# Attention scores by blocks of 64 tokens with both heads on 128 partitions, in a fused attention and expert kernel

## The chip, the cores and the metric

One core of a Trainium2 chip. The time is device time in microseconds of one launch, median of several runs. TensorE is called PE in the profile, its weight loads PEld, VectorE DVE, ScalarE ACT, GpSimd POOL, SyncE SP.

## The reference

```python
def _attn_ref(q, k, v):                       # 4 x 8 heads x 576 tokens x 64, float32
    scores = 1/sqrt(64) * q @ k.T
    mask = (pos[:, None] // 64) >= (pos[None, :] // 64)
    scores = np.where(mask, scores, -1e9);  scores -= scores.max(-1)
    attn = np.exp(scores);  attn /= attn.sum(-1) + 1e-9
    return attn @ v
x = attention as 2304 tokens x 512
x = leaky_relu(x @ w_in, 0.01) @ w_out        # 512 x 2048, 2048 x 512
out = top-1 of 8 experts with a skip score    # w1 512 x 1024, w2 1024 x 512 each
```

A token sees all tokens of its own block of 64 and of the blocks before it. 576 tokens are nine blocks.

## The kernel before

The kernel has four stages: attention, into which the first quarter of the first layer ("half a", 512 of 2048 hidden columns) is woven; the rest of that layer; routing with the first expert; the other experts. The change is in the attention (`class Attention`, lines 28 to 285) and in the due times of the steps woven into it (line 448).

The attention works on 16 pairs of heads, four pairs for each of four batch entries. For a pair, `load` brings q, k and v with tokens on partitions (tiles `qn`, `kn`, `vn`; five tiles of 128 tokens, the last half full). `prep` turns k and q with TensorE (`transposes`, lines 89 to 95; the last 64 tokens by a transpose of 64 rows and columns) into PSUM tile `big`; ACT copies k (line 98), DVE copies q times the scale (line 113). Head 0 stands on partitions 0 to 63, head 1 on 64 to 127. POOL copies the last 64 tokens of q into the diagonal quarters of `qd`, zero elsewhere (line 116).

`s_steps` makes the scores. `products` (line 126) takes a tile of 128 query tokens j = 0 to 3 against 128 (j + 1) keys, one float32 matmul per head with 64 rows of contraction; each is two MATMUL instructions. A small bf16 product adds -1e30 where the first 64 queries would see the last 64 keys (line 133). `soft` takes the row maximum (DVE, line 143) and the exponential with its sum (ACT, line 144), `norm` divides (DVE, then POOL, line 152). `rest` (line 177) does the last 64 tokens, both heads at once, with `qd` and K of 128.

`t_steps` transposes the probabilities P by 128x128 (line 205), copies them out of PSUM by turns with ACT and DVE (line 207; tile `ph`), and multiplies with the values (`mm`, line 241: per head 64 output partitions, tile `pv`); `fin` splits the result in two float32r halves in `xT`. Steps with g = 0 cover tokens 0 to 255, with g = 1 tokens 256 to 575.

Order: `steps` (line 256) gives each step a due time, two units to a pair; the transposes and values of a pair come `1 + lag` = 2.3 units behind its scores, so that neighbouring pairs overlap. The steps of half a and the splitting of its weights (`split64`) have due times of their own, and line 466 runs all in order of due time. A planner then orders each engine's instructions by a simulated timeline; `keep_in_program_order` ties an instruction behind the one traced before it on its engine. PSUM tags: `ps` has four banks (scores and transposed P), `mm` two (values, half a), `big` one double bank.

Of the kernel before, what the change touches and what calls it, by code (L numbers as in the profile page):

```python
# [27 lines left out]
class Attention:  # L28
# [3 lines left out]

    MASK = -1e30

    def __init__(self, tc, ctx, q, k, v, ident, ps, side, place):
        nc = self.nc = tc.nc  # L40
        self.q, self.k, self.v, self.ident, self.ps = q, k, v, ident, ps
        self.B, self.H, self.S, self.D = q.shape
        S = self.S
        self.nt = nt = S // 128
        self.pool = ctx.enter_context(tc.tile_pool(name="at", bufs=2, side=side))
        fix = ctx.enter_context(tc.tile_pool(name="afix", bufs=1, side=side))

        self.nat = [fix.tile([128, 5, 2, 64], F32, name=nm) for nm in ("qn", "kn")]
        self.qT, self.kT = ([place[:, S * i : S * i + S] for i in at] for at in ((0, 1), (2, 3)))
        self.mask = [fix.tile([128, n], BF16, name=nm) for nm, n in (("who", 128), ("mask", 64))]  # L50
        nc.vector.memset(self.mask[0], 0.0)
        for h in range(2):
# [8 lines left out]
        self.P2 = []
        for i in range(2):
            self.P2.append([fix.tile([128, 2, 128 * (j + 1)], F32, name=f"P{j}_{i}") for j in range(nt)])
            t = fix.tile([128, 128 * (nt + 1)], F32, name=f"P{nt}_{i}")
            nc.gpsimd.memset(t[:, S:], 0.0)
            self.P2[i].append(t)
# [16 lines left out]
    def prep(self, p, nat):  # L83
        nc, S = self.nc, self.S
        qn, kn = nat
        qT, kT, qd = self.qT[p % 2], self.kT[p % 2], self.qd[p % 2]
        st = dict(qT=qT, kT=kT, qd=qd, vs=self.vn[p % 3])

        def transposes(src):
            pt = self.ps.tile([128, 1024], F32, name="big", bufs=1)  # L90
            f = src.rearrange("p t h d -> p t (h d)")
            for t in range(4):
                nc.tensor.transpose(pt[:, t * 128 : (t + 1) * 128], f[:, t], self.ident)  # L93
            nc.tensor.transpose(pt[:, 512:576], f[0:64, 4], self.ident[0:64, 0:64])
            return pt[:, 0:S]

        def s_k():
            nc.scalar.copy(kT, transposes(kn))

        def s_q():  # L100
            if p:
                parts = [(transposes(qn), 0, S)]
            else:
                f = qn.rearrange("p t h d -> p t (h d)")
                parts = []
                for i0, i1 in ((0, 512), (512, S)):
                    pt = self.ps.tile([128, 512], F32, name="pq", tag="mm", bufs=2)
                    for t in range(i0 // 128, -(-i1 // 128)):
                        m = min(128, i1 - 128 * t)
                        nc.tensor.transpose(pt[:, 128 * t - i0 : 128 * t - i0 + m], f[0:m, t], self.ident[0:m, 0:m])  # L110
                    parts.append((pt[:, 0 : i1 - i0], i0, i1))
            for pt, i0, i1 in parts:
                nc.vector.tensor_scalar(out=qT[:, i0:i1], in0=pt, scalar1=self.D ** -0.5, scalar2=None, op0=ALU.mult)
            for h in range(2):
                r = slice(64 * h, 64 * h + 64)
                nc.gpsimd.tensor_copy(qd[r, r], qT[r, S - 64 : S])

        return st, [s_k, s_q]

    def s_steps(self, p, st, g):  # L120
# [5 lines left out]
        def products(sp, j, c0):  # L126
            n = 128 * (j + 1)
            for h in range(2):
                r = slice(64 * h, 64 * h + 64)
                nc.tensor.matmul(sp[h][:, c0 : c0 + n], st()["qT"][r, 128 * j : 128 * j + 128], st()["kT"][r, 0:n], start=True, stop=False)  # L130
            for h in range(2):
                r = slice(64 * h, 64 * h + 64)
                nc.tensor.matmul(sp[h][:, c0 + n - 64 : c0 + n], self.mask[0][r], self.mask[1][r], start=False, stop=True)  # L133
# [20 lines left out]
        def pair():  # L154
            return [self.ps.tile([128, 512], F32, name="sp", tag="ps", bufs=4) for _ in range(2)]

        def both():
            sp = pair()
            st_ = stat("both", 4)
            for j in range(2):  # L160
                products(sp, j, 128 * j)
            for j in range(2):
                for h in range(2):
                    soft(Ps[j][:, h], sp[h][:, 128 * j : 128 * j + 128 * (j + 1)], st_, 2 * j + h)
            norm([Ps[i][:, h] for i in range(2) for h in range(2)], st_)

        def one(j):
            n = 128 * (j + 1)
            sp = pair()
            products(sp, j, 0)  # L170
            st_ = stat(f"one{j}", 2 if j < self.nt - 1 else 3)
            for h in range(2):
                soft(Ps[j][:, h], sp[h][:, 0:n], st_, h)
            if j < self.nt - 1:
                norm([Ps[j][:, i] for i in range(2)], st_)

        def rest():

            n, S = self.S // 2, self.S
            sp = self.ps.tile([128, 1024], F32, name="big", bufs=1).rearrange("p (a c) -> p a c", a=2)  # L180
            for a in range(2):
                nc.tensor.matmul(sp[:, a, 0:n], st()["qd"], st()["kT"][:, a * n : a * n + n], start=True, stop=True)  # L182
            P = Ps[self.nt][:, 0:S]
            j = self.nt - 1
            st_ = stat(f"one{j}", 3)
            soft(P.rearrange("p (a c) -> p a c", a=2), sp[:, :, 0:n], st_, 2, AX.XY)
            norm([Ps[j][:, i] for i in range(2)] + [P], st_)

        if g == 0:
            return [both]  # L190
        return [lambda j=j: one(j) for j in range(2, self.nt)] + [rest]

    def t_steps(self, p, st, g, xh, xl):
# [3 lines left out]
        last = Ps[self.nt]  # L197
# [14 lines left out]
        def four(jc):  # L212

            js = (2 * g, 2 * g + 1)
            turn(lambda pt: [(pt[:, (2 * h + i) * 128 : (2 * h + i + 1) * 128], Ps[j][:, h, jc * 128 : jc * 128 + 128])
                             for h in range(2) for i, j in enumerate(js)],
                 lambda t, pt: (t[:, jc, :, 0:256], pt.rearrange("p (h c) -> p h c", h=2)), "ad"[jc % 2])

        def second():
            turn(lambda pt: [(pt[:, h * 128 : h * 128 + 128], Ps[1][:, h, 128:256]) for h in range(2)],  # L220
                 lambda t, pt: (t[:, 1, :, 128:256], pt[:, 0:256].rearrange("p (h c) -> p h c", h=2)), "d")

        def fourth():
            def todo(pt):
                v = pt[:, 0:384].rearrange("p (h c) -> p h c", h=2)
                return [(v[:, h, 0:128], Ps[3][:, h, 384:512]) for h in range(2)] + [(v[:, :, 128:192], last[:, 384:512])]
            turn(todo, lambda t, pt: (t[:, 3, :, 0:192], pt[:, 0:384].rearrange("p (h c) -> p h c", h=2)), "a")
# [5 lines left out]
        if g == 0:  # L233
            turns = [lambda: four(0), second]

            runs = [(0, 0, slice(0, 256), 0), (1, 1, slice(128, 256), 128)]
        else:
            turns = [lambda jc=jc: four(jc) for jc in range(3)] + [fourth, lasts]
            runs = [(jc, jc, slice(0, 320), 0) for jc in range(3)] + [(3, 3, slice(0, 192), 128), (4, 3, slice(256, 320), 256)]

        def mm(run):
            jc, i, cs, c0 = run
            if jc == 0:
                box["pv"] = self.ps.tile([128, 512], F32, name="pv", tag="mm", bufs=2)
# [9 lines left out]
        return [alloc] + turns + [lambda run=run: mm(run) for run in runs] + [fin]  # L254

    def steps(self, dst, lag):
# [17 lines left out]
        for p in range(pairs):  # L274
# [14 lines left out]
def attention_moe_kernel(  # L289
# [158 lines left out]
    for u, (t0, t1, n) in enumerate(((10.35, 17.15, 7), (17.15, 19.1, 4), (21.5, 26.2, 7), (26.35, 33.1, 7))):  # L448
# [277 lines left out]
    lag = 2  # L726
# [628 lines left out]
```

## Time and profile before

| | |
|---|---|
| median of 3 runs | 803.55 us (801.63 to 805.36) |
| profiled execution | 804.18 us, span 802.4 us |
| mean granted clock of TensorE | 0.984 |
| PE busy | 762.4 us (95%), 4526 instructions |
| PEld, DVE, ACT, POOL busy | 579.9, 426.3, 331.7, 309.3 us |
| chain that ended last | PE 78%, DVE 12%, DMA 3% |

Busy time of PE is that of overlapping, pipelined matmuls: an instruction's own duration is longer than its distance to the next one. The price of an instruction in a full stream is the distance between starts. A row `MATMUL sp<-wbt 64*128 64x384` has 64 rows of contraction, 128 columns of the stationary operand and 384 columns that stream; `x4` counts instructions merged into the row.

### The profile page before, as it was taken

To read this page: it belongs to the slowest core of one execution; us is meant where nothing else is said; L and a number is where in the kernel's file an instruction comes from. 1 tells how busy PE (TensorE), PEld (TensorE's weight loads), DVE (VectorE), ACT (ScalarE), POOL (GpSimd) and SP (SyncE) were. 2 spreads that over 40 slices of the span, in tenths; PEclk is the share of its full clock that TensorE was granted. 3 is DMA by queue.
4 is the path that set the end of the run, shared out by engine and by line. 5 is a ranking of instruction groups with operands and counts; after the bars stand their busy time and mean duration, and the time that the engine had idled before them with its cause. 6 is when DMAs were issued, how large, how long until landed. Compare 5 with 4: busy or idle time off the path is not lost.

```text
span 802.4 us, 12709 instructions
## 1 busy us (share of the span) xinstructions
PE 762.4 (95%) x4526; PEld 579.9 (72%) x4527; DVE 426.3 (53%) x1030; ACT 331.7 (41%) x783; POOL 309.3 (39%) x427
## 2 busy tenths in 40 slices
PE   4799999999999999999999999999999998899995
PEld 2456776777766769899989998878899976674441
DVE  2786554454535664576574299996912365221121
ACT  3786555564545665555454222122222251111221
POOL 2785442343424352554344333435332452201011
PEclk8799999999999999999999999999999999999998
DMA  7464622262122031662224356302302221999630
GB/s 170 120 177 104 177 46 71 58 176 72 45 81 48 16 106 40 213 231 82 86 79 158 79 158 197 119 26 93 119 2 79 54 91 30 311 348 388 238 128 14
DMA packets 101108, 96.91 MB, mean 121 GB/s; under 512 B 69198, under 2 KB 72270, under 8 KB 101042
## 3 DMA queue, kind: packets, MB, share of 16 engines
q1 hardware_dynamic: 93778, 82.58, 33.2%
q0 software_dynamic: 7264, 13.50, 5.7%
q8 instruction: 36, 0.59, 0.3%
q14 instruction: 30, 0.25, 0.1%
HBM read 74.38 MB, written 21.98 MB: 120 GB/s over the span
## 4 chain that ended last, share of the span: by engine, by line
PE 78%; DVE 12%; DMA 3%; issue 2%; ACT 2%; SPq 2%; POOL 1%; POOLq 0%; DVEq 0%; ACTq 0%
PE ph L389 21%; PE acc L389 13%; PE sp L130 7%; PE po L389 7%; DVE xlast L608 6%; PE pv L246 6%; PE pt L205 5%; PE ph L1119 3%; PE pp L1133 3%; PE big L182 2%; PE py L861 2%; PE big L93 2%; PE ph L861 1%; DMA list<-li,sli 1%; DVE u L380 1%
## 5 line engine op out<-in xcount | busy, mean ns | idle before, releaser
L389 PE MATMUL ph<-xT,wbt 128*128 128x384 f32 x864 | 167.1, 338 | 4.2 <-DVE u L380 3.1
L389 PEld LDWEIGHTS ph<-xT,wbt 128*128 128x128 f32 x864 | 151.8, 188 | 14.0 <-DVE u L380 5.1
L381 POOL TENSOR_TENSOR gl<-u,gh 128x384 fp32r<-128x384 f32 x72 | 80.4, 1117 | 138.9 <-ACT gh L380 130.9
L389 PE MATMUL acc<-wbt,gh 128*128 128x512 f32 x432 | 131.9, 394 | 0.0
L152 POOL TENSOR_SCALAR P<-P,stat 128x128 f32<-128x128 f32 (+2 forms) x144 | 81.4, 584 | 88.2 <-DVE stat L150 69.2
L389 PEld LDWEIGHTS acc<-wbt,gh 128*128 128x128 f32 x432 | 79.7, 188 | 12.0
L380 ACT CAST gh<-u 128x384 fp32r<-128x384 f32 x72 | 37.0, 514 | 120.8 <-DVE u L380 52.0
L389 PE MATMUL acc<-wbt,gl 128*128 128x512 f32 x216 | 82.1, 396 | 0.0
L143 DVE TENSOR_REDUCE stat<-sp 128x1 f32<-128x128 f32 (+3 forms) x128 | 60.1, 485 | 40.6 <-PE sp L133 28.8
L144 ACT ACTIVATE P<-sp,stat 128x128 f32<-128x128 f32 (+3 forms) x128 | 67.5, 531 | 28.3 <-DVE stat L143 27.4
L380 DVE TENSOR_TENSOR u<-ph,u 128x384 f32<-128x384 f32 x72 | 39.7, 551 | 70.4 <-ACT u L379 70.2
L130 PE MATMUL sp<-wbt 64*128 64x128 f32 (+3 forms) x256 | 72.4, 496 | 1.2 <-ACT P L144 0.7
L379 ACT ACTIVATE u<-ph 128x384 f32<-128x384 f32 x72 | 35.3, 490 | 63.9 <-PE ph L389 55.8
L205 PE MATMUL pt<-ident,P 128*128 128x128 f32 x400 | 60.0, 282 | 0.2 <-ACT P L144 0.2
L360 POOL TENSOR_TENSOR cv<-cv,cv 128x512 int32<-128x512 int32 x32 | 41.5, 1297 | 44.8 <-DVE cv L359 32.7
L389 PE MATMUL ph<-xT,wia 128*128 128x384 f32 x288 | 57.3, 344 | 0.0
L246 PE MATMUL pv<-ph,vn 128*64 128x320 f32 (+4 forms) x448 | 53.6, 367 | 2.1 <-ACT ph L207 1.2
L205 PEld LDWEIGHTS pt<-ident,P 128*128 128x128 f32 x400 | 45.4, 142 | 13.9 <-issue 8.6
L389 PE MATMUL po<-woa,gA 128*128 128x512 f32 x216 | 54.6, 400 | 0.0
L608 DVE CUSTOM_DVE_ANT_0 xlast<-x,raw 128x512 f32<-128x512 f32 x72 | 53.7, 785 | 0.0
L389 PEld LDWEIGHTS ph<-xT,wia 128*128 128x128 f32 x288 | 49.1, 188 | 4.0 <-issue 0.9
L389 PEld LDWEIGHTS po<-woa,gA 128*128 128x128 f32 x216 | 39.4, 188 | 11.6 <-issue 1.8
(264 smaller groups left out, 1120.7 us busy)
## 6 DMA issues: line engine op xcount, KB each, us to landing
wbt<-in_moe_w_dram SPq DMA_DIRECT2D x40, 512.0 KB
raw<-in_moe_w_in_dram SPq DMA_DIRECT2D x16, 512.0 KB
raw<-in_moe_w_out_dram SPq DMA_DIRECT2D x16, 512.0 KB
xTd<-xT POOLq DMA_DIRECT2D x4, 1152.0 KB
part_d<-cv SPq DMA_DIRECT2D x18, 256.0 KB
x<-part_d SPq DMA_DIRECT2D x6, 768.0 KB
xT<-xTd POOLq DMA_DIRECT2D x6, 768.0 KB
out_dram<-x SPq DMA_DIRECT2D x6, 768.0 KB
```

The costliest lines, as they stand in the source:

```text
L130: nc.tensor.matmul(sp[h][:, c0 : c0 + n], st()["qT"][r, 128 * j : 128 * j + 128], st()["kT"][r, 0:n], start=True, stop=False)
L143: nc.vector.tensor_reduce(out=st_[:, 1, i : i + 1], in_=sv, op=ALU.max, axis=ax, negate=True)
L144: nc.scalar.activation(out=P, in_=sv, func=AF.Exp, bias=st_[:, 1, i : i + 1], accum_out=st_[:, 0, i : i + 1])
L152: nc.gpsimd.tensor_scalar(out=P, in0=P, scalar1=rs[:, i : i + 1], scalar2=1.0, op0=ALU.mult, op1=ALU.mult)
L205: nc.tensor.transpose(o, src, self.ident)
L246: nc.tensor.matmul(box["pv"][64 * h : 64 * h + 64, c0:N], st()["vs"][:, jc, h], box["ph"][:, i, h, cs], start=(jc == 0), stop=(jc == runs[ ...
L360: nc.gpsimd.tensor_tensor(out=w, in0=w, in1=low, op=ALU.add)
L379: nc.scalar.activation(out=u, in_=ph, func=AF.Copy, scale=0.01)
L380: return [nc.vector.tensor_tensor(out=u, in0=ph, in1=u, op=ALU.max), nc.scalar.copy(gh, u), nc.gpsimd.tensor_tensor(out=gl, in0=u, in1=gh. ...
L381: nc.gpsimd.tensor_tensor(out=gl, in0=u, in1=gh.bitcast(F32), op=ALU.subtract)]
L389: nc.tensor.matmul(ps, x, y, start=first and m == 0, stop=last and m == 3 * n - 1)
L608: nc.vector.tensor_tensor_reduce(out=junk, in0=x2[:, t], in1=wrow[j], scale=1.0, scalar=0.0, op0=ALU.mult, op1=ALU.add, accum_out=box["L"] ...
```

## The change

The scores are made by blocks of 64 queries. `qd` now holds all nine blocks of q: block i has head 0's 64 queries in columns 0 to 63 on partitions 0 to 63, head 1's in columns 64 to 127 on partitions 64 to 127, and zeros in the other quarters. One matmul with 128 rows of contraction gives both heads' scores of block j, on 128 partitions, against exactly 64 (j + 1) keys: no mask. The scaled q goes there from PSUM by DVE (head 0) and ACT (head 1); the q tile without zeros and POOL's copies are gone. P tiles hold a block of both heads, padded with zeros to a multiple of 128 columns where needed. The last tokens of q and k are turned by whole 128x128 transposes (the empty half of the tiles is zeroed once). The copy of the fourth key tile of P goes from ACT to DVE. The values of both parts run together after all of a pair's transposes, pinned in program order, at a later due time for all pairs but the first four; the products of blocks 0 to 3 are pinned too; the values of g = 0 have a bank of `ps` in place of `mm`. The steps of half a's second and fourth unit get later due times.

```diff
+        self.pin = tc.keep_in_program_order
+        self.nb = S // 64
...
+        self.kT = [place[:, S * i : S * i + S] for i in range(2)]
+        self.qd = [place[:, 2 * S * i : 2 * S * i + 2 * S].rearrange("p (i c) -> p i c", c=128) for i in (1, 2)]
+        for t in self.nat[::-1]:
+            nc.gpsimd.memset(t[64:128, 4], 0.0)
+        for t, eng in zip(self.qd, (nc.vector, nc.gpsimd)):
+            for h in range(2):
+                eng.memset(t[64 * h : 64 * h + 64, :, 64 - 64 * h : 128 - 64 * h], 0.0)
+        self.P2 = []
+        for i in range(2):
+            self.P2.append([fix.tile([128, 128 * (j // 2 + 1)], F32, name=f"P{j}_{i}") for j in range(self.nb)])
+            for j in range(0, self.nb, 2):
+                nc.gpsimd.memset(self.P2[i][j][:, 64 * (j + 1) :], 0.0)
...
+        kT, qd = self.kT[p % 2], self.qd[p % 2]
+        st = dict(kT=kT, qd=qd, vs=self.vn[p % 3])
...
-            for t in range(4):
+            for t in range(5):
                 nc.tensor.transpose(pt[:, t * 128 : (t + 1) * 128], f[:, t], self.ident)
-            nc.tensor.transpose(pt[:, 512:576], f[0:64, 4], self.ident[0:64, 0:64])
...
+                        nc.tensor.transpose(pt[:, 128 * t - i0 : 128 * t - i0 + 128], f[:, t], self.ident)
...
+            sc = self.D ** -0.5
             for pt, i0, i1 in parts:
-                nc.vector.tensor_scalar(out=qT[:, i0:i1], in0=pt, scalar1=self.D ** -0.5, scalar2=None, op0=ALU.mult)
-            for h in range(2):
-                r = slice(64 * h, 64 * h + 64)
-                nc.gpsimd.tensor_copy(qd[r, r], qT[r, S - 64 : S])
+                for h in range(2):
+                    r = slice(64 * h, 64 * h + 64)
+                    o, i_ = qd[r, i0 // 64 : i1 // 64, r], pt[r].rearrange("p (i c) -> p i c", c=64)
+                    if h:
+                        nc.scalar.activation(out=o, in_=i_, func=AF.Copy, scale=sc)
+                    else:
+                        nc.vector.tensor_scalar(out=o, in0=i_, scalar1=sc, scalar2=None, op0=ALU.mult)
...
+        def product(o, j, c0, n):
+            pin = self.pin if j < 4 else lambda ins: ins
+            pin(nc.tensor.matmul(o, st()["qd"][:, j], st()["kT"][:, c0 : c0 + n], start=True, stop=True))
...
+        def blocks(js, name, w, k0, done=()):
+            sp = self.ps.tile([128, 512], F32, name="sp", tag="ps", bufs=4)
+            st_ = stat(name, w)
+            at = [sum(64 * (i + 1) for i in js[:m]) for m in range(len(js) + 1)]
+            for m, j in enumerate(js):
+                product(sp[:, at[m] : at[m + 1]], j, 0, 64 * (j + 1))
+            for m, j in enumerate(js):
+                soft(Ps[j][:, 0 : 64 * (j + 1)], sp[:, at[m] : at[m + 1]], st_, k0 + m)
+            if done:
+                norm([Ps[j][:, 0 : 64 * (j + 1)] for j in done], st_)
...
+                product(sp[:, a, 0:n], j, a * n, n)
+            P = Ps[j][:, 0:S]
...
+            norm([Ps[i][:, 0 : 64 * (i + 1)] for i in (j - 2, j - 1)] + [P], st_)
...
-            return [both]
-        return [lambda j=j: one(j) for j in range(2, self.nt)] + [rest]
+            return [lambda: blocks((0, 1, 2), "a", 4, 0), lambda: blocks((3,), "a", 4, 3, range(4))]
+        return [lambda: blocks((4,), "b", 2, 0), lambda: blocks((5,), "b", 2, 1, (4, 5)),
+                lambda: blocks((6,), "c", 3, 0), lambda: blocks((7,), "c", 3, 1), rest]
...
+        def some(bs, jc, c0, eng):
+            n = len(bs)
+            def copy(t, pt):
+                d = t[:, jc, :, c0 : c0 + 64 * n].rearrange("p h (i c) -> p i h c", c=64)
+                return d, pt[:, 0 : 128 * n].rearrange("p (i h c) -> p i h c", h=2, c=64)
+            turn(lambda pt: [(pt[:, m * 128 : m * 128 + 128], Ps[j][:, jc * 128 : jc * 128 + 128]) for m, j in enumerate(bs)], copy, eng)
...
-            turns = [lambda: four(0), second]
+            turns = [lambda: some((0, 1, 2, 3), 0, 0, "a"), lambda: some((2, 3), 1, 128, "d")]
...
-            turns = [lambda jc=jc: four(jc) for jc in range(3)] + [fourth, lasts]
+            turns = [lambda jc=jc: some((4, 5, 6, 7), jc, 0, "ada"[jc]) for jc in range(3)] + [lambda: some((6, 7, 8), 3, 0, "d"), lasts]
...
-                box["pv"] = self.ps.tile([128, 512], F32, name="pv", tag="mm", bufs=2)
+                box["pv"] = self.ps.tile([128, 512], F32, name="pv", tag=("ps", "mm")[g], bufs=(4, 2)[g])
             for h in range(2):
-                nc.tensor.matmul(box["pv"][64 * h : 64 * h + 64, c0:N], st()["vs"][:, jc, h], box["ph"][:, i, h, cs],
-                                 start=(jc == 0), stop=(jc == runs[-1][0]))
+                self.pin(nc.tensor.matmul(box["pv"][64 * h : 64 * h + 64, c0:N], st()["vs"][:, jc, h], box["ph"][:, i, h, cs],
+                                          start=(jc == 0), stop=(jc == runs[-1][0])))
...
-        return [alloc] + turns + [lambda run=run: mm(run) for run in runs] + [fin]
+        return [alloc] + turns, lambda: [mm(run) for run in runs], fin
...
-                put(t + cut[g] + 1 + lag, t + cut[g + 1] + 1 + lag, self.t_steps(p, st, g, *dst(p, g)))
+            (a0, m0, f0), (a1, m1, f1) = (self.t_steps(p, st, g, *dst(p, g)) for g in range(2))
+            put(t + 1 + lag, t + 2.8 + lag, a0 + a1)
+            at = t + 2.8 + lag if p < self.H // 2 else t + 4.85
+            out += [(at, lambda m0=m0, m1=m1: (m0(), m1())), (at, lambda f0=f0, f1=f1: (f0(), f1()))]
...
-    for u, (t0, t1, n) in enumerate(((10.35, 17.15, 7), (17.15, 19.1, 4), (21.5, 26.2, 7), (26.35, 33.1, 7))):
+    for u, (t0, t1, n) in enumerate(((10.35, 17.15, 7), (18.95, 20.05, 4), (21.5, 26.2, 7), (26.95, 33.1, 7))):
```

## Rows read from the trace of the kernel before

**Rows 1.** Busy time of each engine, clock and DMA in stretches of the span.

```profile
core 0: us, PE busy (x) PEld busy (x) DVE busy (x) ACT busy (x) POOL busy (x), PEclk, DMA share, GB/s
42.70:59.00 16.30, 14.69 (x91) 9.48 (x89) 14.15 (x29) 14.10 (x37) 13.51 (x17) 0.90 0.58 168
59.00:72.00 13.00, 13.00 (x93) 8.27 (x95) 9.44 (x25) 9.56 (x29) 8.63 (x14) 1.00 0.50 125
...
85.80:308.60 222.80, 222.35 (x1390) 156.02 (x1390) 115.43 (x266) 124.71 (x334) 86.10 (x146) 1.00 0.31 83
```

**Rows 2.** Timeline of PE over one pair: start, us until the last end, merged instructions.

```profile
58.89 2.27 PE L246 MATMUL pv<-ph,vn 128*64 128x320 f32 x20
61.10 0.44 PE L205 MATMUL pt<-ident,P 128*128 128x128 f32 x2
61.37 0.60 PE L93 MATMUL big<-ident,kn 128*128 128x128 f32 x4
61.90 0.27 PE L94 MATMUL big<-ident,kn 64*128 64x64 f32 x1
62.10 0.65 PE L246 MATMUL pv<-ph,vn 128*64 128x256 f32 x4
62.69 0.92 PE L130 MATMUL sp<-wbt 64*128 64x384 f32 x4
...
63.56 0.66 PE L205 MATMUL pt<-ident,P 128*128 128x128 f32 x4
64.15 0.44 PE L246 MATMUL pv<-ph,vn 128*64 128x128 f32 x4
64.52 1.12 PE L130 MATMUL sp<-wbt 64*128 64x512 f32 x2
...
65.60 0.65 PE L93 MATMUL big<-ident,qn 128*128 128x128 f32 x4
66.19 0.27 PE L94 MATMUL big<-ident,qn 64*128 64x64 f32 x1
66.19 1.12 PE L130 MATMUL sp<-wbt 64*128 64x512 f32 x2
...
67.28 1.42 PE L205 MATMUL pt<-ident,P 128*128 128x128 f32 x11
68.53 1.14 PE L182 MATMUL big<-wbt,qd 128*128 128x288 f32 x4
69.50 0.60 PE L205 MATMUL pt<-ident,P 128*128 128x128 f32 x4
70.03 0.48 PE L130 MATMUL sp<-wbt 64*128 64x128 f32 x2
...
71.35 0.66 PE L205 MATMUL pt<-ident,P 128*128 128x128 f32 x4
71.94 1.30 PE L246 MATMUL pv<-ph,vn 128*64 128x320 f32 x8
```

**Rows 3.** Timeline of PE in a later pair: seven transposes and what follows.

```profile
238.51 0.93 PE L205 MATMUL pt<-ident,P 128*128 128x128 f32 x7
239.28 1.14 PE L182 MATMUL big<-wbt,qd 128*128 128x288 f32 x4
```

**Rows 4.** Chain that ended last, in order of time: long runs of values.

```profile
58.96 2.20 PE pv L246 x20
...
308.63 2.21 PE pv L246 x20
```

**Rows 5.** Groups by line and shape, 0 to 420 us: busy, mean ns, idle before.

```profile
L98 ACT COPY wbt<-big 128x576 f32<-128x576 f32 x16 | 10.2, 639 | 12.5 <-PE big L94 12.4
...
L207 ACT COPY ph<-pt 128x384 f32<-128x384 f32 x16 | 7.7, 484 | 0.6 <-PE pt L205 0.6
...
L207 DVE COPY ph<-pt 128x512 f32<-128x512 f32 x32 | 21.9, 685 | 13.3 <-PE pt L205 13.2
...
L116 POOL COPY qd<-wbt 64x64 f32<-64x64 f32 x32 | 7.7, 240 | 33.6 <-DVE wbt L113 28.9 <-PE ph L389 3.7
```

More of the change, by code (lines that the diff above doesn't have):

```diff
@@ L28 @@
 class Attention:
-    MASK = -1e30
     def __init__(self, tc, ctx, q, k, v, ident, ps, side, place):
         nc = self.nc = tc.nc
+        self.pin = tc.keep_in_program_order
         self.q, self.k, self.v, self.ident, self.ps = q, k, v, ident, ps
@@ L43, in __init__ @@
         S = self.S
-        self.nt = nt = S // 128
+        self.nb = S // 64
+        self.nt = S // 128
         self.pool = ctx.enter_context(tc.tile_pool(name="at", bufs=2, side=side))
@@ L48, in __init__ @@
         self.nat = [fix.tile([128, 5, 2, 64], F32, name=nm) for nm in ("qn", "kn")]
-        self.qT, self.kT = ([place[:, S * i : S * i + S] for i in at] for at in ((0, 1), (2, 3)))
-        self.mask = [fix.tile([128, n], BF16, name=nm) for nm, n in (("who", 128), ("mask", 64))]
-        nc.vector.memset(self.mask[0], 0.0)
-        for h in range(2):
-            nc.vector.memset(self.mask[0][64 * h : 64 * h + 1, 0:64], 1.0)
-        nc.vector.memset(self.mask[1], self.MASK)
-        self.qd = [fix.tile([128, 128], F32, name=f"qd{i}") for i in range(2)]
-        self.vn = [fix.tile([128, 5, 2, 64], F32, name=f"vn{i}") for i in range(3)]
-        for t in self.qd:
-            nc.gpsimd.memset(t, 0.0)
+        self.vn = [fix.tile([128, 5, 2, 64], F32, name=f"vn{i}") for i in range(3)]
+        self.kT = [place[:, S * i : S * i + S] for i in range(2)]
[10 more added lines that the diff above has]
+                nc.gpsimd.memset(self.P2[i][j][:, 64 * (j + 1) :], 0.0)
         for t in self.vn:
             nc.gpsimd.memset(t[64:128, 4], 0.0)
[L61 to L66, printed above, removed]
     def load(self, p, which):
@@ L85, in prep @@
         qn, kn = nat
-        qT, kT, qd = self.qT[p % 2], self.kT[p % 2], self.qd[p % 2]
-        st = dict(qT=qT, kT=kT, qd=qd, vs=self.vn[p % 3])
+        kT, qd = self.kT[p % 2], self.qd[p % 2]
+        st = dict(kT=kT, qd=qd, vs=self.vn[p % 3])
         def transposes(src):
@@ L108, in s_q @@
                     for t in range(i0 // 128, -(-i1 // 128)):
-                        m = min(128, i1 - 128 * t)
-                        nc.tensor.transpose(pt[:, 128 * t - i0 : 128 * t - i0 + m], f[0:m, t], self.ident[0:m, 0:m])
+                        nc.tensor.transpose(pt[:, 128 * t - i0 : 128 * t - i0 + 128], f[:, t], self.ident)
                     parts.append((pt[:, 0 : i1 - i0], i0, i1))
+            sc = self.D ** -0.5
             for pt, i0, i1 in parts:
-                nc.vector.tensor_scalar(out=qT[:, i0:i1], in0=pt, scalar1=self.D ** -0.5, scalar2=None, op0=ALU.mult)
-            for h in range(2):
-                r = slice(64 * h, 64 * h + 64)
-                nc.gpsimd.tensor_copy(qd[r, r], qT[r, S - 64 : S])
+                for h in range(2):
[5 more added lines that the diff above has]
+                        nc.vector.tensor_scalar(out=o, in0=i_, scalar1=sc, scalar2=None, op0=ALU.mult)
         return st, [s_k, s_q]
@@ L124, in s_steps @@
         box = {}
[L126 to L133, printed above, removed]
+        def product(o, j, c0, n):
+            pin = self.pin if j < 4 else lambda ins: ins
+            pin(nc.tensor.matmul(o, st()["qd"][:, j], st()["kT"][:, c0 : c0 + n], start=True, stop=True))
         def stat(name, w):
@@ L152, in norm @@
                 nc.gpsimd.tensor_scalar(out=P, in0=P, scalar1=rs[:, i : i + 1], scalar2=1.0, op0=ALU.mult, op1=ALU.mult)
[L154 to L175, printed above, removed]
+        def blocks(js, name, w, k0, done=()):
[8 more added lines that the diff above has]
+                norm([Ps[j][:, 0 : 64 * (j + 1)] for j in done], st_)
@@ L177, in rest @@
         def rest():
-            n, S = self.S // 2, self.S
+            n, S, j = self.S // 2, self.S, self.nb - 1
             sp = self.ps.tile([128, 1024], F32, name="big", bufs=1).rearrange("p (a c) -> p a c", a=2)
             for a in range(2):
[L182 to L185, printed above, removed]
+                product(sp[:, a, 0:n], j, a * n, n)
@@ L186, in rest @@
+            P = Ps[j][:, 0:S]
+            st_ = stat("c", 3)
             soft(P.rearrange("p (a c) -> p a c", a=2), sp[:, :, 0:n], st_, 2, AX.XY)
-            norm([Ps[j][:, i] for i in range(2)] + [P], st_)
+            norm([Ps[i][:, 0 : 64 * (i + 1)] for i in (j - 2, j - 1)] + [P], st_)
         if g == 0:
-            return [both]
-        return [lambda j=j: one(j) for j in range(2, self.nt)] + [rest]
+            return [lambda: blocks((0, 1, 2), "a", 4, 0), lambda: blocks((3,), "a", 4, 3, range(4))]
@@ L196, in t_steps @@
         Ps = self.P2[p % 2]
-        last = Ps[self.nt]
+        last = Ps[8]
         N = (256, 320)[g]
@@ L210, in alloc @@
             box["ph"] = self.pool.tile([128, 2 + 2 * g, 2, N], F32, name=f"ph{g}", bufs=2)
[L212 to L227, printed above, removed]
+        def some(bs, jc, c0, eng):
[4 more added lines that the diff above has]
+            turn(lambda pt: [(pt[:, m * 128 : m * 128 + 128], Ps[j][:, jc * 128 : jc * 128 + 128]) for m, j in enumerate(bs)], copy, eng)
         def lasts():
```

## Prediction

> **What bounds the kernel now.** I read the table of stretches first. From 59 to 308.6 us, where the attention runs (alone until 85.8, then mixed with products of the first matmul layer), TensorE is never idle for more than half a microsecond in all: 13.00 of 13.00 us, then 222.35 of 222.80, at the full granted clock of 1.00. DVE, ACT and POOL are busy 39 to 74% there. Before 59 us nobody is full: TensorE 14.69 of 16.30, at a mean clock of 0.90, DVE 14.15, ACT 14.10 [rows 1]. So what TensorE saves between 59 and 308.6 us comes off the end; what it saves earlier mostly doesn't.
>
> Busy says nothing of how well TensorE is used, so I read its timeline over one whole pair of heads, from one long run of `pv` products to the next, taking the difference of two starts as the price of a row [rows 2]. There TensorE does nothing but attention. By kind, in us:
> - `pv`: 58.89 to 61.10, 62.10 to 62.69, 64.15 to 64.52: 2.21 + 0.59 + 0.37 = 3.17
> - 25 transposes of P: 0.27 + 0.59 + 1.25 + 0.53 + 0.59 = 3.23
> - 10 transposes of k and q: 0.53 + 0.20 + 0.59 = 1.32 (the second 64-row one starts together with a product)
> - scores of tiles 0 to 3 with masks: 62.69 to 63.56, 64.52 to 65.60, 66.19 to 67.28, 70.03 to 71.35: 0.87 + 1.08 + 1.09 + 1.32 = 4.36
> - scores of the last 64 tokens (`rest`): 0.97
>
> Sum 13.05, which is 71.94 - 58.89.
>
> Two things in it are no arithmetic. First, what stands next to a change of the operand's shape is dear: seven whole transposes among 128-row work take 0.77, 0.110 each [rows 3]; four of them ahead of a 64-row or 64-column instruction or behind one take 0.53 or 0.59 instead of 0.44, and a single 64x64 one takes 0.20 [rows 2]. So each crossing between full shapes and halves costs 0.09 to 0.15. Second, the scores: the two heads stand on halves of the rows, and for 384 columns four instructions take 0.75, which at the rate of `rest` below is little over two of them (0.65), so the heads run together; for 512 columns each head has a stretch of its own of some 0.97 [rows 2].
>
> **The change on TensorE, part by part**, for one pair.
>
> Transposes: 35 whole ones, no 64-row ones. 35 x 0.110 = 3.85, against 3.23 + 1.32 = 4.55. Saved 0.70.
>
> Scores: blocks 0 to 7 need 64 x (1 + ... + 8) = 2304 columns, each matmul as two instructions like `rest`. `rest` has 4 instructions of 288 columns in 0.97, 0.842 ns per column [rows 2]. 4608 columns make 3.88. Block 0 has 64 columns only, 0.054; a new stationary operand of 128x128 can be no cheaper than the 0.110 of a transpose, so 2 x 0.056 more: 3.99. Masks: none. Against 4.36, saved 0.37. That half the rows are now multiplied by zeros costs nothing where the heads ran apart anyway (512 columns), and costs a factor of two in the three smaller sizes; the crossings and the masks pay for that. Block 8 stays 0.97.
>
> With every pair of heads together, no mask and no crossing, the old scores (1280 columns per head) would take 2 x 1280 x 0.842 = 2.16, and the new ones would be 1.83 dearer; as built they take 4.36. The Trainium skill, TensorEngine Tiling (Array Packing), section "Performance Considerations", speaks against the change: with a contraction of 64 or less, use two row tiles, for up to twice the speed. The trace agrees with that for 128 to 384 columns, not for 512.
>
> Values: 20 instructions with 2432 columns in 2.21, leaving the half shape included; the other 8 have 768 columns: at the same 0.909 ns 0.70. In one run 2.91, and 0.15 for the crossing ahead and the first instruction behind: 3.06 against 3.17. Saved 0.11. If the pin keeps the order but other work falls between, up to three crossings stay and some 0.3 is lost again.
>
> Sum: 3.85 + 3.99 + 0.97 + 3.06 = 11.87 against 13.05: 1.18 saved per pair. 14 pairs end behind 59 us (the long `pv` runs from 72 to 308.6, first and last of 15 in the rows) [rows 4]: 16.5 us. Mixed with the other layer's products there are more crossings than in the pair read, so I bound the saving by 0.9 (values still scattered) and 1.4 per pair: 12.6 to 19.6.
>
> **The other engines.** The transposed q goes out by ACT for one head and DVE for the other, each 64 partitions by 576. No row has 64 partitions; the nearest are whole copies of 576 columns, 639 ns on ACT; half of it is the lower end. I take the whole: ACT +0.64. The 384-column copy of P goes from ACT, -0.48, to DVE, between the 0.48 that ACT needs and DVE's 0.69 for 512 columns [rows 5]. The scores' maxima and exponentials stay 8 + 1 each with 2304 columns instead of 2560. POOL loses two copies of 240 ns per pair. ACT +0.16 and DVE +0.55 per pair of 13.05: with the shorter pair ACT goes from 74% to about 82% in 59 to 72 us, DVE from 73 to 84% (9.56 + 0.16 and 9.44 + 0.55 over 11.87). All of it lies beside TensorE, but the room is small there; later, at 52 and 56%, it is wide [rows 1]. I price the covers that fail with 1 us in all.
>
> At the start POOL and DVE zero more tiles: 2 + 2 of q's, 10 of P's, 2 of k and q. They are due before the first transposes and copies and beside the loads; the first 59 us pass with waits for loads and weight splits, so I take 0, with -1 and +2 as ends (a row of POOL's small work, 240 ns, times the eight more that may stand ahead of something).
>
> Moved: the values of the first 256 tokens wait for the whole pair, and for the later pairs all values stand 0.75 of a half-pair step behind the last transpose; the second unit of the first layer starts 1.8 steps later, so nearly a pair's work of TensorE must be filled by attention alone, as it is at 59 to 72 us, without idling. `pv`'s waits are new: behind a waiting `pv`, all that TensorE has queued waits, first the next pair's transposes, and for those DVE and ACT. Now TensorE waits 0.45 us in all over 85.8 to 308.6 [rows 1]; I take 1.5 more, with 0 and 14 x 1.2 as ends. The loads of the next values (SP's queue) come free up to a step later; they are needed two pairs on, so 0.
>
> Sum: -16.5 + 1 + 1.5 = -14, and with 0.12 more for each of the 12 mixed pairs (halfway to 1.4) -15.5. The profiled execution took 804.18, span 802.4 and 1.8 around it, 0.6 above the median 803.55. So 788.
>
> **Rivals.**
> 1. Partial: other engines or the new order hold TensorE up, or the values stay scattered: 0.3 to 0.9 per pair is left, 4 to 12 us, about 795. For it: DVE and ACT at 82 to 84% in the first pairs. Against it: 52 to 56% later.
> 2. Weight loads show: if each new product's 128x128 operand were exposed for another 0.11, as the 64-row work shows at its entries, 18 x 0.11 = 2.0 would be lost per pair; half of that eats 14 of 16.5, about 801. Against: `rest`, of just this shape, has 0.242 per instruction with nothing exposed.
> 3. Slower: the pinned run of values waits for its last copy. Place: the first `pv` of a run, behind the last transposes, which DVE must still copy (0.69). If DVE has one more thing queued, TensorE idles some 1.5 per pair. It decides from 1.18 per pair; at 1.5 over 16 pairs 16 x 0.32 = +5, about 809. Against: only where the order puts no other work between, and for 12 of 16 pairs the due time leaves 0.75 step.
> 4. The lost work of two heads at a time outweighs the crossings: with scores 1.83 dearer and all else as in my sum, a pair loses 1.83 - 0.70 - 0.11 = 1.02: 14 x 1.02 = +14, 818. Against: the 4.36 that the old scores take. The Trainium skill's rule named above would have it so.
>
> **How the numbers follow.** Forecast (11 to 21 us off) 0.55, its own range 783 to 793; rival 1 0.20; rival 2 0.10, half of it within 0.5% of before; rival 3 0.10, a little of it within; rival 4 0.02; other 0.03. 0.5% (4 us) is about what a measurement of this kernel can tell from no change. Faster 0.79, same 0.09, slower 0.12. For 8 in 10 the range leaves out the dear half of rival 2, rivals 3 and 4, and what saves over 23: 781 to 800.
>
> **What would show it.** The long runs of `pv` 11.9 apart where attention stands alone; 28 `pv` instructions in one run of about 3.0; whole transposes at 0.110 everywhere; block 7 (two instructions of 512 columns) at 0.86; the stretch to the last `pv` some 15 shorter, and everything behind it of equal length. Wrong it would be if TensorE shows idle time before `pv` of over 1 per pair, if the granted clock falls between 59 and 308, or if the products of blocks cost over 5 per pair.

## The result and the profile after

The changed kernel takes 783.26 us (median of 4, 781.5 to 784.99) against 803.45 (median of 4) of the kernel before: ratio 0.9748, 95% interval 0.9714 to 0.9783. Run again later it took 784.74, ratio 0.9759 (0.9738 to 0.9781). Forecast were 788, in 781 to 800.

The stretches of the profiled execution (784.99, span 783.2), as [rows 1]:

```profile
0.00:55.10 55.10, 38.36 (x186) 26.66 (x188) 40.68 (x82) 37.07 (x94) 34.54 (x62) 0.94 0.64 167
55.10:67.30 12.20, 12.12 (x86) 8.91 (x87) 10.54 (x26) 9.32 (x27) 7.60 (x11) 1.00 0.55 137
67.30:79.20 11.90, 11.90 (x86) 8.95 (x87) 8.74 (x23) 8.63 (x25) 4.65 (x9) 1.00 0.33 76
79.20:288.40 209.20, 207.41 (x1316) 163.66 (x1316) 114.35 (x282) 125.23 (x337) 78.16 (x126) 1.00 0.32 88
288.40:325.00 36.60, 35.88 (x189) 31.52 (x189) 18.57 (x38) 19.19 (x37) 16.66 (x43) 1.00 0.43 129
```

TensorE is still the full engine, and the clock stays at 1.00. Idle grew from 0.45 to 1.79 us in the mixed stretch. Where attention runs alone DVE is busy 10.54 of 12.20 and 8.74 of 11.90 us, ACT 9.32 and 8.63: fuller than before, and not full.

The timeline of PE over one pair, to be laid beside [rows 2]:

```profile
67.24 2.92 PE L217 MATMUL pv<-ph,vn 128*64 128x256 f32 x28
70.09 0.70 PE L122 MATMUL sp<-wbt 128*128 128x256 f32 x2
70.63 0.60 PE L183 MATMUL pt<-ident,P 128*128 128x128 f32 x4
71.07 0.60 PE L85 MATMUL big<-ident,kn 128*128 128x128 f32 x4
71.50 0.38 PE L183 MATMUL pt<-ident,P 128*128 128x128 f32 x2
71.72 0.27 PE L85 MATMUL big<-ident,kn 128*128 128x128 f32 x1
71.83 1.35 PE L122 MATMUL sp<-wbt 128*128 128x320 f32 x4
73.02 0.60 PE L183 MATMUL pt<-ident,P 128*128 128x128 f32 x4
73.45 0.92 PE L122 MATMUL sp<-wbt 128*128 128x448 f32 x2
74.21 0.71 PE L85 MATMUL big<-ident,qn 128*128 128x128 f32 x5
74.75 1.04 PE L183 MATMUL pt<-ident,P 128*128 128x128 f32 x8
75.63 1.02 PE L122 MATMUL sp<-wbt 128*128 128x512 f32 x2
76.49 0.93 PE L183 MATMUL pt<-ident,P 128*128 128x128 f32 x7
77.25 1.14 PE L122 MATMUL big<-wbt 128*128 128x288 f32 x4
78.22 0.94 PE L122 MATMUL sp<-wbt 128*128 128x64 f32 x6
79.09 1.14 PE L217 MATMUL pv<-ph,vn 128*64 128x256 f32 x10
```

From start to start of the two long runs: 11.85 us; the sum had 11.87. (The pair ahead of it took 12.20.) There is one `128*64` row in it where [rows 2] have three, and no `64*128`. Transposes cost 0.11 each beside anything. Blocks 0 to 7 cost 0.87 + 0.54 + 1.19 + 0.76 + 0.86 = 4.22 (0.09 of the 0.87 is the way into the values), `rest` 0.97, the run of values 2.85.

Chain that ended last, as [rows 4]:

```profile
55.11 2.86 PE pv L217 x28
...
288.42 2.21 PE pv L217 x20
```

The new copies, as [rows 5] (line and shape, count, busy, mean ns):

```profile
L110 DVE TENSOR_SCALAR wbt<-big 64x576 f32<-64x576 f32 x15 | 11.1, 739 | 2.2 <-PE big L85 2.0
L108 ACT ACTIVATE wbt<-big 64x576 f32<-64x576 f32 x15 | 9.7, 647 | 3.9 <-DVE wbt L110 3.5
L185 DVE COPY ph<-pt 128x384 f32<-128x384 f32 x16 | 8.8, 550 | 3.0 <-PE pt L183 2.9
```

Half the partitions cost the whole price: 647 ns for 64x576 on ACT, against 639 for 128x576 [rows 5], and 739 on DVE, where the copy of q on 128 partitions (L113 of the kernel before, 15 times) took 749.

For all kernels one stretch is compared below, where TensorE sets the pace: from the start of the last `pv` instruction of the second pair to that of the last pair, in the one profiled execution of each kernel. Before it is 60.9 to 310.6, 249.7 us; after 57.7 to 290.4, 232.7, so 17.0 of the 19.2 us that the spans differ by. The start gave 3.2, and behind the attention 1.0 went back (491.8, then 492.8). In the repeated run the stretch is 232.1, and the second pair ends at 60.0: the stretch repeats well, the start does not.

### The profile page after: what moved, and what is told of

Same layout as the page of the kernel before. It is cut to its first block, busy times and chain, and to the rows that moved or that the text cites. A ratio compares the mean times of both kernels' runs of the same rounds, so it can differ in the third digit from the quotient of the medians.

```text
span 783.2 us, 12449 instructions
## 1 busy us (share of the span) xinstructions
PE 744.1 (95%) x4398; PEld 591.2 (75%) x4399; DVE 429.4 (55%) x1044; ACT 332.1 (42%) x784; POOL 298.5 (38%) x405
## 4 chain that ended last, share of the span: by engine, by line
PE 72%; DVE 18%; DMA 3%; ACT 2%; issue 2%; SPq 2%; POOL 0%; POOLq 0%; DVEq 0%; ACTq 0%
PE ph L363 19%; PE acc L363 12%; DVE xlast L582 9%; PE sp L122 7%; PE po L363 6%; PE pv L217 5%; PE pt L183 4%; PE ph L1093 3%; PE pp L1107 3%; PE py L835 2%; PE big L122 2%; PE big L85 2%; PE ph L835 1%; DVE u L354 1%; DMA raw<-in_moe_w_in_dram 1%
## 5 line engine op out<-in xcount | busy, mean ns | idle before, releaser
L355 POOL TENSOR_TENSOR gl<-u,gh 128x384 fp32r<-128x384 f32 x72 | 80.3, 1116 | 141.7 <-ACT gh L354 137.7
L141 POOL TENSOR_SCALAR P<-P,stat 128x448 f32<-128x448 f32 (+4 forms) x144 | 76.0, 545 | 114.5 <-DVE stat L139 50.2
L122 PE MATMUL sp<-wbt 128*128 128x64 f32 (+7 forms) x256 | 83.4, 437 | 3.0 <-DVE ph L185 1.2
L132 DVE TENSOR_REDUCE stat<-sp 128x1 f32<-128x64 f32 (+7 forms) x128 | 57.0, 451 | 43.5 <-PE sp L122 34.0
L133 ACT ACTIVATE P<-sp,stat 128x64 f32<-128x64 f32 (+7 forms) x128 | 64.2, 505 | 22.7 <-DVE stat L132 20.3
L183 PEld LDWEIGHTS pt<-ident,P 128*128 128x128 f32 x400 | 48.5, 142 | 21.5 <-issue 7.1
L183 PE MATMUL pt<-ident,P 128*128 128x128 f32 x400 | 57.9, 275 | 4.9 <-DVE xT L223 2.1
L363 PE MATMUL po<-woa,gA 128*128 128x512 f32 x216 | 59.5, 416 | 0.0
L122 PEld LDWEIGHTS sp<-wbt 128*128 128x128 f32 x256 | 41.0, 201 | 9.1 <-DVE ph L185 2.1
```

What stands on the lines that cost most here:

```text
L122: pin(nc.tensor.matmul(o, st()["qd"][:, j], st()["kT"][:, c0 : c0 + n], start=True, stop=True))
L132: nc.vector.tensor_reduce(out=st_[:, 1, i : i + 1], in_=sv, op=ALU.max, axis=ax, negate=True)
L133: nc.scalar.activation(out=P, in_=sv, func=AF.Exp, bias=st_[:, 1, i : i + 1], accum_out=st_[:, 0, i : i + 1])
L141: nc.gpsimd.tensor_scalar(out=P, in0=P, scalar1=rs[:, i : i + 1], scalar2=1.0, op0=ALU.mult, op1=ALU.mult)
L183: nc.tensor.transpose(o, src, self.ident)
L355: nc.gpsimd.tensor_tensor(out=gl, in0=u, in1=gh.bitcast(F32), op=ALU.subtract)]
```

## The experiments

A visit is here a run of instructions in a half shape (`64*128`: row; `128*64`: column) between others, counted in the list of TensorE's instructions over the stretch. Idle is TensorE's, in the stretch. The ratio is to the kernel before, run beside each. "Second pair" is the time at which the stretch begins, with the mean granted clock up to it.

| kernel | median | ratio (95%) | second pair (clock) | stretch | row visits | column visits | idle |
|---|---|---|---|---|---|---|---|
| before | 803.45 | | 60.9 (0.86) | 249.7 | 71 | 41 | 0.5 |
| after | 783.26 | 0.9748 (0.9714 to 0.9783) | 57.7 (0.94) | 232.7 | 0 | 15 | 1.9 |
| e9 after again | 784.74 | 0.9759 (0.9738 to 0.9781) | 60.0 (0.91) | 232.1 | 0 | 15 | 1.5 |
| e1 extra half product | 816.55 | 1.0150 (1.012 to 1.018) | 61.4 (0.92) | 259.8 | 101 | 15 | 0.3 |
| e2 extra full product | 792.31 | 0.9867 (0.984 to 0.9895) | 58.7 (0.94) | 240.3 | 0 | 15 | 0.8 |
| e3 half-shape last transposes | 786.59 | 0.9799 (0.9771 to 0.9828) | 58.0 (0.91) | 237.4 | 24 | 15 | 1.3 |
| e4 values apart | 804.84 | 1.0017 (0.9997 to 1.0037) | 60.2 (0.94) | 252.1 | 0 | 55 | 6.4 |
| e5 before, whole transposes | 803.53 | 1.0000 (0.9983 to 1.0016) | 63.1 (0.84) | 247.5 | 54 | 41 | 0.7 |
| e6 before, values in one run | 794.35 | 0.9873 (0.985 to 0.9895) | 64.7 (0.82) | 233.7 | 56 | 16 | 1.3 |
| e7 scores by blocks alone | 808.27 | 1.0055 (1.0038 to 1.0072) | 61.0 (0.92) | 255.9 | 23 | 55 | 6.3 |
| e8 unpinned | 789.28 | 0.9803 (0.9782 to 0.9825) | 57.2 (0.94) | 237.7 | 0 | 27 | 3.4 |
| e10 after, loads ahead | 781.93 | 0.9757 (0.973 to 0.9784) | 57.6 (0.91) | 232.2 | 0 | 15 | 2.0 |
| e11 before, loads ahead | 807.57 | 1.0055 (1.0038 to 1.0073) | 65.5 (0.84) | 249.0 | 72 | 41 | 0.5 |
| e12 values in two runs | 785.66 | 0.9766 (0.9736 to 0.9797) | 56.6 (0.94) | 236.7 | 0 | 29 | 1.4 |

**e1 and e2: does the shape cost, or the instruction?** In `product`, with r = 0:64 in e1 and 0:128 in e2:

```diff
+ if j < 8:
+     pin(nc.tensor.matmul(o[:, 0:64], self.extra[0][r], self.extra[1][r], start=True, stop=True))   # bf16 zeros
  pin(nc.tensor.matmul(o, st()["qd"][:, j], ...))
```

> The changed kernel, and ahead of each of the products of blocks 0 to 7 one bf16 product more with 64 rows of contraction and 64 columns, of zeros, into the bank that the block's own product then overwrites. Theory of crossings (what the change saves is the price of passing between full and 64-row shapes): each one costs its own 0.06 and two crossings of 0.09 to 0.15, some 0.25, so 8 x 0.25 = 2.0 per pair and, over the 14 to 16 pairs in which TensorE sets the end, +28 to +32: 811 to 815 us, slower than the kernel before. Rival (the arithmetic counts, crossings are hidden behind other instructions): 8 x 0.06 = 0.5 per pair, +7: 790 us, the same as the next run.

> The same with 128 rows of contraction in the added bf16 products, so that no shape changes; the number of instructions is the same. Both theories: 8 x 0.06 to 0.11 per pair (its own 64 columns, or the load of its weights), +7 to +14: 790 to 797 us. If it is as slow as the run with 64 rows, the added instruction is what costs, and not the shape.

Measured: +33 and +9 us over the first run of the changed kernel, as the theory of crossings had it (e1 1.5 above its range). The two differ by 19.5 us in the stretch over 101 visits, so a visit of the half shape costs 0.19 more than an instruction of the full one. The added full product itself costs 7.6 to 8.2 us over as many, 0.08 each. The timeline of PE in e1:

```profile
63.35 0.27 PE L88 MATMUL big<-ident,kn 128*128 128x128 f32 x1
63.56 0.20 PE L127 MATMUL sp<-exb,exa 64*128 64x64 bf16 x1
63.69 0.81 PE L128 MATMUL sp<-wbt 128*128 128x320 f32 x2
64.42 0.20 PE L127 MATMUL sp<-exb,exa 64*128 64x64 bf16 x1
64.56 0.91 PE L128 MATMUL sp<-wbt 128*128 128x384 f32 x2
```

The transpose ahead of the visit takes 0.21 in place of 0.11, the visit 0.13.

**e3: the last transposes in the half shape again.**

```diff
- for t in range(5):
+ for t in range(4):
      nc.tensor.transpose(pt[:, t * 128 : (t + 1) * 128], f[:, t], self.ident)
+ nc.tensor.transpose(pt[:, 512:576], f[0:64, 4], self.ident[0:64, 0:64])
...   # and the same where q is turned in two parts
```

> The changed kernel with the last 64 tokens of k and q turned by transposes of 64 rows and columns again, nothing else undone. Crossings: two visits of the half shape per pair, each 0.19 to 0.25 above a whole transpose, 0.4 to 0.5 per pair, +5 to +8: 788 to 791 us. Rival (a quarter of the work is a quarter of the work): not slower, 780 to 784 us.

The median is 1.4 below the expected range, though not in the rival's. The stretch is 4.7 to 5.3 longer (against the two runs of the changed kernel) with 24 row visits, 0.20 to 0.22 each above a whole transpose: crossings.

**e4: the values apart.**

```diff
- put(t + 1 + lag, t + 2.8 + lag, a0 + a1)
- ... values and fin of both parts at one due time, pinned
+ for g in range(2):
+     put(t + cut[g] + 1 + lag, t + cut[g + 1] + 1 + lag, self.t_steps(p, st, g, *dst(p, g)))   # unpinned, tag "mm"
```

The lines are shortened. The later due times of half a's units stay.

> The changed kernel with the values of the two parts of a pair apart again, each behind its own transposes with the due times of before, unpinned, in the banks of before. Crossings: four more entries and exits per pair, 0.2 to 0.5: +3 to +8, 786 to 791 us. Rival (values ready earlier keep TensorE better fed than one late run): 775 to 783 us.

A wide miss: 804.84, the whole gain gone, +20 to +22 instead of +3 to +8. The timeline of PE over one of its pairs:

```profile
61.51 0.71 PE L85 MATMUL big<-ident,qn 128*128 128x128 f32 x5
62.15 0.65 PE L217 MATMUL pv<-ph,vn 128*64 128x256 f32 x4
62.73 0.81 PE L122 MATMUL sp<-wbt 128*128 128x320 f32 x2
63.47 0.44 PE L217 MATMUL pv<-ph,vn 128*64 128x128 f32 x4
63.84 0.91 PE L122 MATMUL sp<-wbt 128*128 128x384 f32 x2
...
70.36 0.77 PE L85 MATMUL big<-ident,qn 128*128 128x128 f32 x5 [0.29 <-ACT wbt L89]
71.06 2.16 PE L217 MATMUL pv<-ph,vn 128*64 128x320 f32 x16
73.15 1.04 PE L122 MATMUL sp<-wbt 128*128 128x64 f32 x6
74.12 0.34 PE L217 MATMUL pv<-ph,vn 128*64 128x64 f32 x4
```

The planner now puts pieces of values between the products, four visits in this pair, and splits even the long run (x16, then x4 behind the next products). And TensorE waits (engine, line, waited for: us, times, longest):

```profile
PE big L85 <- ACT wbt L89: 3.8, 11, 0.9
PE pv L217 <- DVE ph L185: 2.6, 2, 2.3
```

**e12: one more visit, nothing else**, to tell the price of a visit from the disorder of e4.

```diff
- out += [(at, lambda: (m0(), m1())), (at, lambda: (f0(), f1()))]
+ out += [(at - 0.4, m0), (at - 0.4, f0), (at, m1), (at, f1)]   # shortened
```

> The changed kernel with the values of a pair in two pinned runs, the first part's 0.4 of a half-pair step ahead of the second's, other work between them: one more visit of the half shape (128 rows, 64 columns) per pair, 16 in all, nothing else undone. Theory (a visit of that shape costs 0.30 to 0.35 of TensorE's time, entry, exit and the slower first instructions counted, read from the runs before): 15 x 0.30 to 0.35 = 4.5 to 5.3 us from the second pair's end to the last one's, 787 to 791 us. Rival (the 20 us of the kernel with the values apart come from the order and the waits that it made, and a visit costs 0.1 or less): 0 to 1.5 us there, 783 to 786 us.

The stretch is 4.0 to 4.6 longer with 14 more visits, at or a little under the lower end of the 4.5 to 5.3 expected, and well off the rival's 0 to 1.5: 0.29 to 0.33 per visit. The median, 785.66, lies in the rival's range, 0.9 to 2.4 above the changed kernel's two. In the profiled execution the start makes up the difference: the second pair ended at 56.6, 1 to 3 us sooner than in the two of the changed kernel. The start moves by as much between those two. So the price rests on the stretch. The timeline shows what a visit is made of:

```profile
64.29 0.49 PE L183 MATMUL pt<-ident,P 128*128 128x128 f32 x3
64.71 0.87 PE L217 MATMUL pv<-ph,vn 128*64 128x256 f32 x8
65.52 0.66 PE L183 MATMUL pt<-ident,P 128*128 128x128 f32 x4
66.01 1.14 PE L122 MATMUL big<-wbt 128*128 128x288 f32 x4
```

Three transposes take 0.42 (+0.09). The eight values take 0.81, where in the one run they add 0.64 (28 in 2.85 after, 20 in 2.21 before): +0.17. The four transposes behind take 0.49 (+0.05). Together 0.31.

**e5, e6, e7: one part alone.** e5 is the kernel before with the diff of e3 turned round; e6 the kernel before with the diff of e4 turned round, pins of the values and the later due times of half a's units included; e7 has the diffs of e3 and e4 together, so the scores by blocks alone, though with the pinned products and the later units that e4 keeps too.

> The kernel before with the last 64 tokens of k and q turned whole, nothing else. Crossings: two visits of the half shape less per pair, but those that stand next to a 64-row product save only one side: 0.2 to 0.5 per pair, -3 to -8: 796 to 800 us. Rival (no crossing cost, two transposes with more columns): 803 to 805 us.

> The kernel before with the values of both parts of a pair in one pinned run, with the changed due times of values and of the two units, nothing else. Crossings: 0.1 to 0.5 per pair less, -2 to -8: 796 to 802 us. Rival (the pinned run waits for its last copy, and the later units leave TensorE without work): 805 to 812 us.

> The changed kernel with both others undone, so scores by blocks alone: 64-row transposes of the last tokens, values apart. If the three parts add up, this is 783 plus what the two undone parts cost one by one. My sum gave the scores 0.37 per pair and the crossings that go with them the larger part of the transposes' 0.70, some 0.8 of 1.18: -11 to -14, 789 to 793 us. Rival (the heads' concurrency is worth as much as the crossings): 800 to 806 us.

e5 missed: no change in the time, as its rival had it. The stretch is 2.2 shorter with 17 row visits less, and the start gave as much back (second pair at 63.1). e6 did more than expected, -9, with a stretch 16.0 shorter, a start 3.8 longer and 2.0 more behind the attention. e7 missed on the other side, by more than e4 and beyond its rival: alone, the scores by blocks make the kernel slower, by 0.55%, with a stretch 6.2 longer and 5.8 more idle. No run has scores by blocks and values apart with the units' earlier due times, so part of what e4 and e7 lose may come from those.

Laid side by side, the stretches tell the parts apart. The run of values (with its due times) is worth 16.0 on the kernel before and 19.4 to 20.0 on the changed one. The scores by blocks cost 6.2 on the kernel before (e7), and 3.7 where the values stand in one run already (e6 233.7, e3 237.4). The whole last transposes then bring 4.7 to 5.3. So e6 is within 1.0 to 1.6 us of the changed kernel in the stretch. It loses ahead of the stretch: its second pair ends at 64.7, the changed kernel's at 57.7 and 60.0, which is 7.0 and 4.7 of the 8.9 and 7.6 us between the profiled spans.

**e8: no pins.**

```diff
- self.pin = tc.keep_in_program_order
+ self.pin = lambda ins: ins
```

> The changed kernel with no products or values pinned in program order; due times as they are. If the pin holds the run of values together against the planner: values scattered, two to four more crossings per pair, +3 to +8, 786 to 791 us. Rival (the due times do it by themselves): 782 to 785 us.

Within the expectation: 12 more column visits, idle 1.5 to 1.9 more, stretch 5.0 to 5.6 longer. So the due times keep most of the run together and the pin the rest.

**e9, e10, e11: the first 59 us.** The changed kernel again; then with two tiles for the natural q and k each; the kernel before with two for q.

```diff
- self.nat = [... for nm in ("qn", "kn")]          # e10
+ self.nat = [... for nm in ("qn0", "qn1", "kn0", "kn1")]
- qn, kn = self.nat
+ qn, kn = self.nat[p % 2 :: 2]
```

> The changed kernel again, so that the next runs have it on the same chip: 781 to 785 us.

> The changed kernel with two tiles each for the natural q and k, so that the loads of the next pair don't wait for this pair's transposes on SP's queue, and with them not the loads of the weights that stand behind. Theory (the first 59 us went 3.9 us faster because the transposes of q freed the tile sooner and SP's queue moved on): more of the same, the first pairs 2 to 6 us earlier, 777 to 781 us. Rival (the first pairs are set by DVE's and ACT's work on weights, not by the queue): 782 to 785 us.

> The kernel before with two tiles for the natural q (k keeps one). Theory of the queue: the third load of weights is issued some 4 us sooner than at 37.35 us and the second pair ends 2 to 4 us earlier than 58.9: 799 to 801 us. Rival (DVE's and ACT's work sets the first pairs): 802 to 805 us, though the loads are issued sooner.

SP's queue of e11 and of the kernel before, the load of the third set of weights:

```profile
25.07 7.97 SPq L340 DMA_DIRECT2D raw<-in_moe_w_out_dram  x3
```

```profile
37.35 1.92 SPq L340 DMA_DIRECT2D raw<-in_moe_w_out_dram  x3
```

The first of the three loads is issued 12 us sooner, the last some 6 us, and the second pair ends later (65.5, not 60.9). The median, 807.57, lies above the theory's range and the rival's. e10, at 781.93, lies between its two ranges; its ratio is that of e9 within their intervals, and its second pair ends at 57.6, beside the 57.7 of the changed kernel's first profile. So loads that are issued sooner did not shorten the start, and the theory of the queue falls.

The traces do show a place where the start was won. In the kernel before, TensorE (first two rows) waits twice for what ACT and DVE bring:

```profile
19.05 1.11 PE L93 MATMUL big<-ident,qn 128*128 128x128 f32 x4 [5.89 <-ACT wbt L98]
25.29 2.26 PE L182 MATMUL big<-wbt,qd 128*128 128x288 f32 x4 [4.83 <-DVE wbt L113]
16.70 0.66 ACT L355 ACTIVATE cv<-raw 128x512 int32<-128x512 uint32 x1 [4.76 <-DMA raw<-in_moe_w_in_dram]
18.36 0.63 ACT L98 COPY wbt<-big 128x576 f32<-128x576 f32 x1
```

In the changed one:

```profile
15.40 0.71 PE L85 MATMUL big<-ident,qn 128*128 128x128 f32 x5
20.82 2.29 PE L122 MATMUL big<-wbt 128*128 128x288 f32 x4 [4.70 <-ACT wbt L108]
13.99 0.64 ACT L89 COPY wbt<-big 128x576 f32<-128x576 f32 x1 [0.36 <-PE big L85]
16.49 0.67 ACT L329 ACTIVATE cv<-raw 128x512 int32<-128x512 uint32 x1 [1.28 <-DMA raw<-in_moe_w_in_dram]
```

In the kernel before, ACT's copy of k (L98) stands behind a step that splits weights (L355) and waits 4.76 us for their load; q's transposes wait with it. In the changed kernel the planner put the copy (L89) ahead of that step, and the first `rest` starts 4.5 us sooner. The order is that of the kernel before in e5, e6 and e11 too, and that of the changed kernel in all with scores by blocks but e1 and e2. In the four kernels with the old scores the second pair ends at 60.9 to 65.5, at a mean granted clock of 0.82 to 0.86 until then; in the ten others at 56.6 to 61.4, at 0.91 to 0.94. How much of the later end and of the lower clock comes from this order, no run shows.

## Why the prediction was right

*TensorE sets the end, a pair costs 11.87.* Right: 11.85 in the pair read. The stretch became 17.0 shorter (17.6 in the repeat), 1.21 per pair over 14 pairs; the sum had 16.5 and, with 1.4 more for the mixed pairs and 2.5 given back to covers and waits, 15.5. Idle grew by 1.4 (1.1 in the repeat), not 2.5.

*Where it comes from.* The prediction's own way of pricing, the distance from one start to the next, can be summed by kind over the whole stretch, with the waits apart:

| kind, us in the stretch | before | after | change | in the sum |
|---|---|---|---|---|
| transposes | 60.3 | 51.0 | -9.3 | -9.8 |
| scores of blocks 0 to 7, masks | 54.6 | 48.8 | -5.8 | -5.2 |
| values | 44.1 | 40.1 | -3.9 | -1.5 |
| `rest` | 13.9 | 12.3 | -1.6 | 0 |
| products of the other layer | 76.4 | 78.6 | +2.2 | 0 |
| idle | 0.5 | 1.9 | +1.4 | +2.5 |

Transposes and scores came out as sized. The values brought 2.4 more; `rest` and the other layer's products, which the sum left alone, moved by -1.6 and +2.2, and the mixed pairs' -1.4 has no row of its own. That these largely cancel is luck.

Priced by visits, 71 row visits at 0.20 (e1 against e2, e3) and 26 column visits at 0.30 (e12) would make 22.0, an estimate; the dearer products and the idle go against it, and the counts don't settle it closer than to a few us. The products are dearer by less than a factor of two: of the old scores' 100 pairs of head instructions in the stretch only 41 start within 12 ns of each other. The others start apart, not only at 512 columns as I read from one pair, but in 35 of the 74 smaller pairs too.

*Zeros and the lost concurrency.* Rival 4 is out as a forecast: blocks 0 to 7 take 4.2 in the pair read, less than the 4.36 of before. Its mechanism is there, though: taken by themselves the scores by blocks made the stretch 3.7 to 6.2 longer (e3 against e6, e7), and the transposes and values paid for that. So neither way of making the scores decides here: e6, with the old half-row scores and the values in one run, has a stretch of 233.7, 1.0 over the changed kernel's. The Trainium skill, TensorEngine Tiling (Array Packing), section "Tiling Modes", says that changing the tiling mode drains the engine. The 0.2 to 0.3 per visit agree with that; no run shows the drain itself.

*Weight loads* (rival 2): blocks 0 to 2 take 0.87 with the way out; nothing shows. *A late run* (rival 3): TensorE waited 1.4 more over 14 pairs, not some 1.5 in each.

*The term that was mis-sized* is the values: "Saved 0.11", "some 0.3 is lost again" if scattered. I priced a `pv` row by its own start and the next one's and booked the rest of its visits with the transposes around it (0.70), and I took the order of other work as given. A column visit costs 0.30, and the planner makes as many as its due times allow: without the run there are 40 more in the stretch (12 us) and 4.5 us of waits (e4). That is 16.5 of 19.4 us; 3 us of e4 stay open. Of e6's 16.0, 15 row and 25 column visits less make 10.5. Its old scores and masks take 8.2 less than in the kernel before (46.4, not 54.6), with 48 pairs of heads side by side and not 41; what of that is the order of work and what the visits stays open. The transposes' 0.70 was in part the values': those of P take 4.8 less in the changed kernel, and 3.3 less in e6 already. The whole last ones alone gave 2.2 in the stretch and nothing in the time (e5), undone they cost 5 (e3).

*The start.* Taken as 0, with -1 and +2: it gave 3.2 in one profile and 0.9 in the other, as far apart as the gain is large. The place is ACT's order of k's copy and the split of weights, shown above, which the prediction didn't look at; how much of the 0.9 to 3.2 it makes is open.

*Behind the attention* all was equal but for 1.0 us.

## What to carry to other kernels

Where TensorE is full, count how often its instructions change between whole and half operands. A visit of a half shape cost 0.2 to 0.3 us here and was in no instruction's own duration, only in the distance of starts. Half-shape work that must stay should be gathered in one run, with due times and pins that keep a planner from scattering it; that was worth the most. Padding to the whole shape paid for a small instruction that stands between whole ones (the last transposes); for the long score products it did not pay by itself. Test a part by taking it away from the finished kernel and by adding it to the old one, and compare stretches beside times: here the times differ by a factor of two (20 and 9 us), the stretches by a fifth (19.4 and 16.0), and the rest is the start and what lies behind.

## What the runs showed of the hardware

A visit of 64-row shape cost 0.19 to 0.22 us more than an instruction of the whole shape (e1 against e2, e3), one of 64 columns 0.29 to 0.33 (e12). Start by start around the first run of 20 values in [rows 2]: the last transpose ahead takes 0.20 in place of 0.11, the first step of the run 0.31 in place of 0.26, its last 0.15 in place of 0.05, and the first transpose behind 0.16 in place of 0.11; so about 0.09 at the way in, 0.10 at the way out, and 0.05 each on the first instruction in the new shape and the first behind. An instruction on 64 partitions took as long as on 128: 647 against 639 ns on ACT, 739 against 749 ns on DVE. Two products on different halves of the rows start 6 to 7 ns apart when they stand side by side; in the kernel before 41 of 100 pairs did.
